# A planned attention and two gated layers on one core: the first gated item's gating, and the second item's products, moved into the attention's written order

## The chip, the cores and the metric

The kernel runs on one core of a Trainium2 chip. TensorE (PE in the profile) multiplies, VectorE (DVE), ScalarE (ACT) and GpSimd (POOL) do the element work, SyncE (SP) issues most of the transfers. The metric is the device time of one execution in microseconds (us); three runs give the median.

## The reference

Causal attention with a forgetting bias, four batches of eight heads, 576 tokens, head size 64; its output (2304 tokens by 512) goes through a sigmoid-gated layer (512 to 1536 and back) and then a cosine-gated layer (512 to 2048 and back). The weights arrive as 64-bit floats.

```python
cum = np.cumsum(np.maximum(s, 0), axis=-1)
bias = -(cum[:, :, :, None] - cum[:, :, None, :])
scores = np.where(causal, -1e9, q @ k.T / 8 + np.minimum(bias, 0))
x = softmax(scores) @ v                                     # 2304 x 512
x = (sigmoid(x @ w_gate) * (x @ w_val)) @ moe_w_out         # d_ff 1536
h = x @ w_in;  out = (h * cos(h)) @ moe2_w_out              # d_ff 2048
```

## The kernel before

**Attention.** The heads are worked in 16 pairs, p = 0 to 15, four pairs to a batch. All its steps are named operations, and one text, `SEQ`, writes them in a single order; each engine runs its own operations in the order in which that text names them, and `:a`, `:d`, `:p` choose ScalarE, VectorE or GpSimd where a step can run on several. `Plan.run` goes through the text once at build time and hands out buffers and PSUM banks with the durations that `add` states; it reorders nothing. The steps of a pair: `GQ`, `GK`, `GV`, `DB` load on SP (`GQT`, `GKT`, `GVT` the last 64 tokens of a whole batch); `PQ`, `PK` transpose on TensorE, `HQ`, `HK` copy that out; `A4`, `A3`, `A2`, `A0`, `A5` are scores; `ZT`, `ZA`, `Z`, `ZM` mask the bias; `X` is bias plus row maximum (VectorE, line 670), `E` the exponential (ScalarE, line 674), `T` and `C` the transposes (TensorE) and their copies (to `pt`); `V0`, `V1` the products with v (lines 744, 746). The sums go through `RA` (GpSimd), `RC` (VectorE), `RT` (TensorE) and `RR` to a row, `RD` stores the row to DRAM, `RB` reads it back spread over all partitions into the one tile `rb`; `U` copies the products of v out, `M` multiplies them by `rb`, and `XH`, `XL` (lines 449/445 and 788) split the result into two halves for the layers.

**Weights.** A piece of 128 by 512 64-bit numbers is fetched by SP into `raw` and turned into a high and a low half by `piece_ops`: exponent (VectorE, then a rebias on ScalarE, line 300), `mant_hi`, `mant_lo`, `sign` (VectorE, then an addition on GpSimd, line 313), `split` (VectorE, then a subtraction on GpSimd, line 321). The three pieces w0, w1, w2 of the first layer's first column block (gate, value, out) are decoded inside the attention's text. There an operation such as `exponent` issues its VectorE and its ScalarE instruction together, so that both stand at the same place of the text.

**Layers.** An item is one column block of 128 for one block of 384 tokens; a product takes three matmuls (`mm3`, lines 366 to 368) and an item's gate and value 24. `gate_val` makes both, `glu` takes the sigmoid (line 843), multiplies (844) and splits (846, 852), `down1` multiplies the item before by its out piece into banks 4 to 7, `evac1` collects. After item i the call `background` issues a share of the decoding of coming pieces: the first call, behind item 0, gives five operations, and the two fetches that they need. Of item 0 the 24 products `I0` to `I7` (three each) stand in the attention's text; its `glu` and all of the items after it come behind the text. The pool `att`, which holds the attention's tiles, is closed before the layers' pools are opened on the same memory.

```python
        attention()
        early.close()
        moe()
```

Of the kernel before, what the change touches and what calls it, by code (L numbers as in the profile page):

```python
# [10 lines left out]
F32 = mybir.dt.float32  # L11
# [58 lines left out]
class Banks(Pool):  # L70


    def pick(self, buf):
        best = (INF, 0, [])
        for i in range(0, self.n, 2):
            a, b = self.free[i], self.free[i + 1]
            if buf.n == 2:
                best = min(best, (max(a, b), 0, [i, i + 1]))
            else:
                for x, y, z in ((a, b, i), (b, a, i + 1)):  # L80
                    best = min(best, (x, -y if y < INF else -1e9, [z]))
        return best[0], best[2]
# [99 lines left out]
warm0 GQ0 tail cum table GKT0 GK0 GQT0 B0 BC0:d PK0 PQ0 Z0.0:p B1 out HQ0:a BC1:a ZT0.0 GK1 HK0:d A4.0 ZA0.0 GQ1 A0.0 X0.1.0 Z1.0:a PK1 DB1 ZT1.0 A3.0 GQ2 ZA1.0 X0.0.0  # L182
X1.1.0 HK1:a ZM1.3.0 X1.0.0 ZM0.3.0 A2.0 E0.1.0 X1.3.0 ZM1.2.0 PQ1 GK2 E1.1.0 E0.0.0 E1.0.0 HQ1:a X0.3.0 T0.1.0 ZT1.1 ZM0.2.0 T0.0.0 Z0.1:p X1.2.0 E1.3.0 ZM0.3.1 A5.0
X0.2.0 A4.1 Z1.1:p GQ3 C0.0.0:d DB2 GK3 ZA1.1 A0.1 E0.3.0 C0.1.0:d T0.3.0 X0.4.0 GV0 ZT0.1 GVT0 GKT4 A3.1 ZA0.1 E1.2.0 ZM1.3.1 E0.2.0 X1.0.1 E0.4.0 C0.3.0:d X0.0.1 T1.3.0
C1.3.0:a X1.1.1 X0.1.1 E0.1.1 PQ2 X0.3.1 ZM0.2.1 RA0 X1.3.1 PK2 HQ2:a T0.4.0 A2.1 E1.0.1 Z1.2:p HK2:d ZM1.2.1 Z0.2:p ZT0.2 ZM0.3.2 E1.1.1 C0.4.0:d E0.0.1 E0.3.1 T0.1.1
T0.0.1 T0.2.0 RC0 A5.1 ZT1.2 X0.2.1 X1.2.1 T1.2.0 X0.4.1 PQ3 C0.1.1:a C0.0.1:a PK3 C0.2.0:a ZA1.2 HQ3:a GQ4 C1.2.0:d A3.2 RT0 HK3:d E1.3.1 A4.2 GV1 T0.3.1 T1.3.1 ZA0.2
RR0:a X0.3.2 ZM1.3.2 E0.4.1 DB3 E1.2.1 X1.3.2 A0.2 X1.0.2 E0.2.1 X0.0.2 X1.1.2 V0.0 ZM1.2.2 X0.1.2 C0.3.1:a C1.3.1:d T0.2.1 E0.0.2 RD0 E1.0.2 T0.4.1 E1.3.2 GQT4 Z1.3:p
V1.0 C0.4.1:d T1.2.1 E1.1.2 T0.0.2 E0.1.2 ZM0.2.2 E0.3.2 U0:d C1.2.1:a ZT0.3 T0.1.2 ZT1.3 GK4 C0.2.1:a A5.2 C0.0.2:a A2.2 RA1 Z0.3:a RC1 A3.3 RB0 X0.4.2 X0.2.2 ZM0.3.3
X1.2.2 T0.3.2 GQ7 T1.3.2 C0.1.2:a ZM1.3.3 GV3 RT1 DB4 X0.3.3 GK5 V0.1 E0.4.2 X1.3.3 ZM1.2.3 ZA0.3 V1.1 ZA1.3 RR1:d M0:d PK4 ZM0.2.3 C1.3.2:d C0.3.2:d T0.4.2 E0.3.3 HK4:d
E1.3.3 U1:a E0.2.2 Z1.4:p PQ4 A4.3 HQ4:d ZT1.4 C0.4.2:a A0.3 X1.0.3 E1.2.2 XH0:p A2.3 Z0.4:p T0.2.2 X0.1.3 E1.0.3 E0.1.3 ZA1.4 X0.0.3 X1.1.3 T1.2.2 X1.2.3 ZM1.3.4 X0.2.3  # L190
T0.3.3 E0.0.3 T1.3.3 E1.1.3 T0.0.3 GV2 ZT0.4 C1.2.2:a ZA0.4 C1.3.3:d ZM0.3.4 C0.2.2:a E0.2.3 C0.3.3:d T0.1.3 A5.3 A3.4 GQT8 GQ5 RD1 X0.4.3 PQ5 RA2 C0.1.3:a C0.0.3:a A4.4
X0.3.4 DB5 A0.4 HQ5:a X1.3.4 E0.4.3 PK5 E0.3.4 V0.2 X1.1.4 X1.0.4 X0.0.4 ZM1.2.4 E1.0.4 RC2 GK6 HK5:d X0.1.4 T0.4.3 GK7 E1.3.4 RT2 RR2:d V1.2 Z1.5:p E1.2.3 E1.1.4
C0.4.3:d E0.1.4 ZM0.2.4 T0.2.3 Z0.5:p T1.2.3 E0.0.4 GQ6 U2:d RB1 A2.4 ZM1.3.5 RD2 T0.1.4 C1.2.3:a T0.0.4 ZT1.5 ZM0.3.5 GVT4 C0.2.3:a ZT0.5 X1.2.4 A5.4 T0.3.4 C0.0.4:a
# [37 lines left out]
def kernel(  # L231
# [847 lines left out]
```

## Time and profile before

| | us |
|---|---|
| median of three runs (1026.04 to 1028.54) | 1027.09 |
| the profiled execution, its own time | 1028.06 |
| its span, first to last instruction | 1026.3 |
| TensorE busy in the span | 1007.6 |
| VectorE, ScalarE, GpSimd busy | 709.7, 475.3, 411.2 |

The profiled execution's time stands 1.8 us above its span and 1.0 us above the median. Busy shares are means over three stages: the attention up to about 168 us, the first layer, and the second. Times in rows are from the span's start.

### The profile page before, as it was taken

What the parts mean: (1) busy time and instruction counts of PE and PEld (TensorE: products, weight loads), DVE (VectorE), ACT (ScalarE), POOL (GpSimd) and SP (SyncE); (2) the same over time, 40 slices, a digit from 0 to 9 for tenths busy, and PEclk for the clock granted to TensorE, in tenths of its full rate; (3) what the DMA queues carried; (4) which work ended last, traced back from release to release, by engine and by line L of the source; (5) the groups of instructions that cost most, each with busy time, mean ns of one, the idle gap of its engine ahead of it and who ended that gap; (6) DMA issues with size and microseconds to landing.
All of it is one profiled execution on the core that took longest, in us unless ns stands there. A gap on an engine that the chain in (4) does not pass through costs nothing.

```text
span 1026.3 us, 17410 instructions
## 1 busy us (share of the span) xinstructions
PE 1007.6 (98%) x6553; PEld 918.4 (89%) x6553; DVE 709.7 (69%) x1365; ACT 475.3 (46%) x1081; POOL 411.2 (40%) x489
## 2 busy tenths in 40 slices
PE   8999997999999999999999999999999999999998
PEld 5666665999999999999999999999999999999997
DVE  7878785655545557643345888987688878886565
ACT  6989894432222222221212335666555455554453
POOL 5478874432212223311112224565255535552222
PEclk9999998999999999999999999999999999999999
DMA  8776752311111112210101111211011101100011
GB/s 192 192 210 173 197 142 74 109 62 42 42 42 42 42 42 82 63 42 21 42 21 42 42 62 42 63 48 55 22 42 57 47 21 42 62 1 26 37 62 61
DMA packets 91508, 69.43 MB, mean 68 GB/s; under 512 B 58848, under 2 KB 79712, under 8 KB 91424
## 3 DMA queue, kind: packets, MB, share of 16 engines
q1 hardware_dynamic: 89792, 67.86, 23.2%
q8 instruction: 51, 0.84, 0.3%
q10 hardware_dynamic: 1632, 0.47, 0.2%
q14 instruction: 33, 0.27, 0.1%
HBM read 63.45 MB, written 4.87 MB: 67 GB/s over the span
## 4 chain that ended last, share of the span: by engine, by line
PE 90%; DVE 2%; DMA 2%; POOL 2%; ACT 2%; issue 1%; SPq 1%; DVEq 0%; POOLq 0%; ACTq 0%
PE pw L366 21%; PE pw L367 21%; PE pw L368 21%; PE pw L926 6%; PE pw L927 6%; PE pw L928 6%; PE pw L634 2%; DMA rb<-rec_d 2%; PE pw L746 1%; PE pw L456 1%; DVE pu L670 1%; ACT pu L674 1%; PE pw L639 1%; PE pw L560 1%; DMA Qn<-in_q_dram 1%
## 5 line engine op out<-in xcount | busy, mean ns | idle before, releaser
L366 PE MATMUL pw<-XH,wp 128*128 128x384 f32 x960 | 324.5, 338 | 5.6 <-ACT tm L843 4.8
L367 PE MATMUL pw<-XL,wp 128*128 128x384 f32 x960 | 324.2, 338 | 0.0
L368 PE MATMUL pw<-XH,wp 128*128 128x384 f32 x960 | 324.1, 338 | 0.0
L321 POOL TENSOR_TENSOR wp<-wm,wp 128x512 fp32r<-128x512 f32 x68 | 101.3, 1490 | 231.5 <-DVE wp L320 230.1
L366 PEld LDWEIGHTS pw<-XH,wp 128*128 128x128 f32 x960 | 181.2, 189 | 10.5 <-ACT tm L843 4.9
L367 PEld LDWEIGHTS pw<-XL,wp 128*128 128x128 f32 x960 | 181.2, 189 | 3.5
L368 PEld LDWEIGHTS pw<-XH,wp 128*128 128x128 f32 x960 | 181.2, 189 | 0.0
L916 POOL TENSOR_TENSOR gl<-tm,gh 128x384 fp32r<-128x384 f32 x96 | 109.3, 1138 | 144.4 <-ACT gh L915 144.3
L313 POOL TENSOR_TENSOR wm<-wm,wx 128x512 int32<-128x512 int32 x68 | 90.5, 1330 | 185.3 <-DVE wm L312 185.2
L844 DVE TENSOR_TENSOR tm<-pw,tm 128x384 f32<-128x384 f32 x72 | 40.1, 557 | 150.1 <-PE pw L368 140.0
L926 PE MATMUL pw<-wp,gh 128*128 128x512 f32 x288 | 112.2, 389 | 0.0
L927 PE MATMUL pw<-wp,gh 128*128 128x512 f32 x288 | 112.1, 389 | 0.0
L928 PE MATMUL pw<-wp,gl 128*128 128x512 f32 x288 | 112.0, 389 | 0.0
L846 ACT CAST gh<-tm 128x384 fp32r<-128x384 f32 x72 | 37.0, 514 | 145.3 <-DVE tm L844 145.3
L901 DVE SCALAR_TENSOR_TENSOR tm<-tm 128x384 f32<-128x384 int32 x96 | 99.2, 1033 | 3.3
L902 ACT ACTIVATE tm<-tm 128x384 f32<-128x384 f32 x96 | 50.5, 526 | 108.5 <-DVE tm L901 108.5
L367 PE MATMUL pw<-gl,wp 128*128 128x384 f32 x288 | 96.8, 336 | 0.0
L366 PE MATMUL pw<-gh,wp 128*128 128x384 f32 x288 | 96.5, 335 | 0.0
L300 ACT ACTIVATE wx<-wx,ebias 128x512 int32<-128x512 int32 x68 | 49.2, 724 | 102.1 <-DVE wx L299 101.0
L368 PE MATMUL pw<-gh,wp 128*128 128x384 f32 x288 | 96.2, 334 | 0.0
L674 ACT ACTIVATE pu<-pu,nm 128x128 f32<-128x128 f32 (+4 forms) x144 | 82.9, 579 | 4.7 <-DVE nm L670 4.4
L909 DVE SCALAR_TENSOR_TENSOR tm<-tm,pw 128x384 f32<-128x384 f32 x96 | 52.7, 549 | 42.4 <-ACT tm L903 42.4
(104 smaller groups left out, 1618.7 us busy)
## 6 DMA issues: line engine op xcount, KB each, us to landing
raw<-in_moe_w_out_dram SPq DMA_DIRECT2D x28, 512.0 KB
CB<-cum_d SPq DMA_DIRECT2D x15, 576.0 KB
raw<-in_moe_w_in_dram SPq DMA_DIRECT2D x16, 512.0 KB
raw<-in_moe_w_gate_dram SPq DMA_DIRECT2D x12, 512.0 KB
raw<-in_moe_w_val_dram SPq DMA_DIRECT2D x12, 512.0 KB
rb<-rec_d SPq DMA_DIRECT2D x32, 144.0 KB
out_dram<-acc SPq DMA_DIRECT2D x17, 256.0 KB
Kn<-in_k_dram SPq DMA_DIRECT2D x16, 256.0 KB
```

The costliest lines, as they stand in the source:

```text
L313: pool.tensor_tensor(m, m, st["x"], ALU.add)
L321: pool.tensor_tensor(w[:, 1], m, f(w[:, 0]), ALU.subtract)
L366: pe.matmul(ps, wh, xh, start=first, stop=False)
L367: pe.matmul(ps, wh, xl, start=False, stop=False)
L368: pe.matmul(ps, wl, xh, start=False, stop=last)
L674: act.activation(o, o, AF.Exp, bias=NMT[nm.slot][:, col:col + 1], scale=-1.0, accum_out=SUMS[sums.slot][:, col:col + 1])
L901: dve.scalar_tensor_tensor(r, kk, -TWO_PI_LO, r, ALU.mult, ALU.add)
L909: dve.scalar_tensor_tensor(g, r, -0.5, h, ALU.add, ALU.mult)
L916: pool.tensor_tensor(gl, g, f(gh), ALU.subtract)
L926: pe.matmul(ps, gh[:, ts], w[:, 0], start=it["first"], stop=False)
L927: pe.matmul(ps, gh[:, ts], w[:, 1], start=False, stop=False)
L928: pe.matmul(ps, gl[:, ts], w[:, 0], start=False, stop=it["last"])
```

## The change

Five edits. (1) `Buf` gets `fix`, so that a buffer can be tied to given banks: items 0 and 1 get banks 0, 1 and 2, 3. (2) The 24 products of item 1 (`I8` to `I15`) and the four gating instructions of item 0 (`Gs`, `Gm`, `Gh`, `Gl`) become operations of the attention's text; their tiles `TMA` and `GPA` lie in the pool `base`, and the layers' rings of tiles count on from there. (3) The decoding of w0, w1, w2 is listed instruction by instruction, with tiles `wx` and `wm` as buffers of the plan. (4) The Q and K tail tiles are one each instead of two. (5) Several stated durations change, and the text `SEQ` is another order throughout, with other choices of engine. In all 16 pairs, copies to `pt` go from 72 on ScalarE and 40 on VectorE to 65 and 47, `HK` from 8 and 8 to 13 and 3, `HQ` from 10 and 6 to 11 and 5, `RR` from 11 and 5 to 7 and 9, `U` from 6 and 10 to 7 and 9, `XL` from 14 on GpSimd and 2 on VectorE to 12 and 4; `M` stays 11 on GpSimd and 5 on VectorE.

```diff
 class Buf:
-    def __init__(self, pool, n=1):
+    def __init__(self, pool, n=1, fix=None):
+        self.fix = fix
...
     def pick(self, buf):
+        if buf.fix is not None:
+            return max(self.free[buf.fix:buf.fix + buf.n]), list(range(buf.fix, buf.fix + buf.n))
...
 SEQ = """
...
-C0.1.15:a GV15 C0.0.15:a RC13 E1.2.14 A3.15 T0.3.14 RT13 T1.3.14 GV14 X0.4.15 RR13:a E0.4.14 T0.2.14 X0.3.15 T1.2.14 A2.15 RD13 X1.3.15 ZM1.2.15 C1.3.14:a I0 ZM0.2.15
-E0.4.15 C0.3.14:d I1 I2 RA14 I3 I4 E0.3.15 X1.2.15 C1.2.14:d RC14 RT14 E1.3.15 X0.2.15 E1.2.15 T0.3.15 M12:p RR14:a w2fetch T1.3.15 C0.2.14:d E0.2.15 RA15 C1.3.15:a
-T0.4.14 T0.4.15 XH12:p C0.4.15:d RB13 XL12:p w2exponent I5 I6 RC15 I7 XL11:d RD14 T0.2.15 M13:d C0.4.14:a w2mant_hi RT15 T1.2.15 C0.3.15:a C0.2.15:a V0.14 w2mant_lo
-RR15:a V1.14 U14:d RD15 w2sign RB14 C1.2.15:a M14:d RB15 w2split V0.15 XH13:p XL13:p V1.15 XH14:a U15:d M15:d XL14:p XH15:d XL15:d
...
+A3.15 X0.1.15 X1.1.15 RB12 X1.0.15 E0.0.15 T1.3.14 I8 X1.3.15 E0.2.14 RA13 I9 E1.1.15 I10 E1.0.15 w1split_lo C0.3.14:d E0.1.15 I11 C1.3.14:a X0.3.15 RC13 T0.1.15 ZM0.2.15
+E0.4.14 RT13 w2mant_hi T0.0.15 RR13:d A5.15 X0.4.15 A2.15 C0.0.15:a RA14 RD13 w2exponent C0.1.15:a T0.2.14 T1.2.14 E1.3.15 M12:p X0.2.15 I0 I1 ZM1.2.15 X1.2.15 I12 I2 I13
+C0.2.14:d I14 E0.2.15 RC14 E0.4.15 T0.4.14 w2rebias w2mant_lo C1.2.14:a RB13 w2sign E0.3.15 GV15 C0.4.14:a RT14 I3 I15 T0.4.15 RR14:d RD14 E1.2.15 T0.2.15 T1.2.15 RA15 I4
+C1.2.15:a M13:p I5 C0.2.15:a I6 RC15 I7 XH11:p RT15 C0.4.15:d T0.3.15 RR15:a w2add_exp T1.3.15 Gs XH13:a w2split_hi C0.3.15:d V0.14 C1.3.15:d V1.14 Gm RD15 XH12:p RB14 Gh
+XL11:p Gl V0.15 V1.15 U14:a M14:p w2split_lo RB15 XH14:d XL14:d U15:a M15:d XH15:p XL12:p XL15:d XL13:d
 """
...
+    TMA = base.tile([P, TB], F32, name="tma")
+    GPA = base.tile([P, 2 * TB], F32R, name="gpa")
...
+        ops = [fetch, exponent, rebias, mant_hi, mant_lo, sign, add_exp, split_hi, split_lo]
+        if single:
+            return ops
...
-            QKT = {x: [att.tile([P, PB, 2, D], F32, name=f"{x}t{i}") for i in range(2)] for x in "QK"}
+            QKT = {x: [att.tile([P, PB, 2, D], F32, name=f"{x}t")] for x in "QK"}
...
+            for i, it in enumerate(items1[0:2]):
+                i_ps = Buf(pl["pw"], 2, 2 * i)
+                i_ps.left += 1
+                for y in range(2 * NDC):
+                    def part(u, z=y // NDC, c=y % NDC, it=it, i_ps=i_ps):
+                        it["ps"] = [PW[:, i_ps.slot + y, 0:it["n"]] for y in range(2)]
+                        xmm(it["ps"][z], W["gv"[z], it["f"]], it["o"], it["n"], [c])
...
+                add("Gs", "act:1780", glu_s, rd=[(i_ps, 0), *[("e", NP - 1, c) for c in range(NS)], *[("e", NP - 2, c) for c in range(NS)]], wr=["g0"])
+                add("Gm", "dve:550", glu_m, rd=[(i_ps, 1)], wr=["g0"])
+                add("Gh", "act:510", glu_h, rd=["g0"], wr=["gh0"])
+                add("Gl", "dve:560", glu_l, rd=["g0", "gh0"], wr=["gl0"])
...
-            TM = mid.tile([P, 5 * TB], F32, name="tm")
-            gp = c2.enter_context(tc.tile_pool(name="gp", bufs=4))
+            TMB = mid.tile([P, 4 * TB], F32, name="tmb")
+            GPB = mid.tile([P, 6 * TB], F32R, name="gpb")
...
             for i, it in enumerate(items1):
+                if i > 1:
+                    gate_val(it)
                 if i > 0:
-                    gate_val(it)
                     for c in range(NDC):
                         down1(items1[i - 1], c)
-                glu(it)
+                    glu(it)
                 if i > 0:
                     evac1(items1[i - 1], 0)
                     evac1(items1[i - 1], 1)
-                glu_lo(it)
                 if i > 0:
+                    glu_lo(it)
```

## Rows read from the trace of the kernel before

**Rows 1.** Windows view, three stretches: engines' busy time, granted TensorE clock, DMA share.

```profile
168.00:172.50 4.50, 0.00 (x0) 0.00 (x0) 1.76 (x3) 2.43 (x3) 1.99 (x3) 0.84 0.25 50
172.50:181.50 9.00, 8.10 (x24) 7.59 (x25) 4.95 (x8) 0.89 (x3) 2.69 (x2) 0.51 0.37 125
...
187.80:560.00 372.20, 372.20 (x2147) 372.20 (x2146) 202.98 (x377) 89.16 (x172) 91.65 (x65) 1.00 0.15 46
```

**Rows 2.** Timeline of TensorE, 166 to 188 us: start, duration, line; idle before.

```profile
167.49 0.28 PE L746 MATMUL pw<-pt,vt 128*64 128x64 f32 x4
172.57 0.69 PE L366 MATMUL pw<-XH,wp 128*128 128x384 f32 x1 [4.79 <-ACT tm L843]
177.61 0.69 PE L366 MATMUL pw<-XH,wp 128*128 128x384 f32 x1 [0.83 <-DVE tm L844]
181.50 0.34 PE L366 MATMUL pw<-gh,wp 128*128 128x384 f32 x1
...
187.74 0.34 PE L366 MATMUL pw<-gh,wp 128*128 128x384 f32 x1
```

**Rows 3.** Windows view, the attention from 16 to 163 us, sum: PE, PEld, DVE, ACT, POOL.

```profile
sum 147.00, PE 140.06 PEld 92.87 DVE 119.63 ACT 131.71 POOL 103.51; mean PE 35.01 PEld 23.22 DVE 29.91 ACT 32.93 POOL 25.88
```

**Rows 4.** Waits of ScalarE, 50 to 100 us, then 140 to 163 us: total, times, longest.

```profile
ACT wx L300 <- DVE wx L299: 2.1, 1, 2.1
...
ACT wx L300 <- DVE wx L299: 1.1, 1, 1.1
```

**Rows 5.** Waits of GpSimd, 16 to 163 us.

```profile
POOL w L776 <- DMA rb<-rec_d: 3.9, 4, 2.1
```

**Rows 6.** Groups by line and form, 0 to 168 us: busy us, mean ns of one.

```profile
L788 POOL TENSOR_TENSOR XL<-w,XH 128x576 fp32r<-128x576 f32 x12 | 17.8, 1485 | 0.8 <-DVE XH L449 0.4
...
L445 ACT COPY pt<-pw 128x384 f32<-128x384 f32 x25 | 11.0, 477 | 0.9 <-PE pw L456 0.7 <-DVE pt L449 0.2
...
L445 ACT COPY K<-pw 128x640 f32<-128x640 f32 x8 | 5.6, 696 | 1.0 <-PE pw L560 0.9
```

**Rows 7.** Timeline of ScalarE, 155 to 174 us and 168 to 192 us.

```profile
162.49 0.25 ACT L445 COPY rr<-pw 9x128 f32<-9x128 f32 x1
...
170.73 1.28 ACT L843 ACT_TABLE_LOAD   x1
...
183.90 0.47 ACT L843 ACTIVATE tm<-pw 128x384 f32<-128x384 f32 x1
```

**Rows 8.** Timeline of SP, 155 to 180 us: issues.

```profile
162.76 0.58 SPq L765 DMA_DIRECT2D rec_d<-rr  x1
...
164.12 7.00 SPq L770 DMA_DIRECT2D rb<-rec_d  x4
177.22 0.38 SPq L295 DMA_DIRECT2D raw<-in_moe_w_gate_dram  x1
```

**Rows 9.** Waits of SP's queue, 165 to 180 us.

```profile
SPq L295 <- DVE XL L788: 6.0, 1, 6.0
...
SPq L770 <- DMA rb<-rec_d: 2.1, 1, 2.1
```

**Rows 10.** Timeline of VectorE, 168 to 192 us.

```profile
169.25 0.76 DVE L776 TENSOR_TENSOR w<-w,rb 128x576 f32<-128x576 f32 x1 [2.68 <-DMA rb<-rec_d]
...
173.89 1.91 DVE L776 TENSOR_TENSOR w<-w,rb 128x576 f32<-128x576 f32 x1 [2.88 <-DMA rb<-rec_d]
...
176.33 0.76 DVE L788 TENSOR_TENSOR XL<-w,XH 128x576 fp32r<-128x576 f32 x1
...
180.68 0.43 DVE L299 TENSOR_SCALAR wx<-raw 128x512 int32<-128x512 int32 x1 [1.86 <-DMA raw<-in_moe_w_gate_dram]
...
185.54 0.56 DVE L852 TENSOR_TENSOR gl<-tm,gh 128x384 fp32r<-128x384 f32 x1 [0.58 <-ACT gh L846]
```

**Rows 11.** The tile rb over the span: count, duration ns min/median/max.

```profile
L776 POOL TENSOR_TENSOR w<-w,rb x11: 1405/1416/1432, 51.8 to 155.5; 128x576 f32<-128x576 f32 x11
L776 DVE TENSOR_TENSOR w<-w,rb x5: 735/758/1909, 34.5 to 173.9; 128x576 f32<-128x576 f32 x5
```

More of the change, by code (lines that the diff above doesn't have):

```diff
@@ new lines @@
+E0.2.10 A2.11 GQT12 GQ12 ZM0.2.11 ZM1.2.11 ZA0.11 X0.1.11 RR9:a X0.0.11 XL6:p T0.2.10 X1.0.11 X1.1.11 E0.0.11 Z1.12:p RB8 w0rebias RA10 T1.2.10 E0.1.11 ZT0.12 V0.9
+C1.2.10:d E1.1.11 C0.2.10:d X1.2.11 V1.9 E1.0.11 PQ12 X0.2.11 T0.1.11 E0.3.11 ZT1.12 U9:d T0.0.11 E1.3.11 HQ12:a A5.11 PQ13 RC10 A3.12 Z0.12:p GK15 C0.1.11:d RD9 E0.2.11
+HQ13:a w1fetch ZA0.12 C0.0.11:d GQ14 X0.4.11 E1.2.11 DB13 ZM1.3.12 ZM0.3.12 T0.3.11 E0.4.11 X0.3.12 RT10 XH7:p RR10:d A4.12 ZA1.12 w0add_exp T1.3.11 XL7:p C0.3.11:a
@@ L287, with piece_ops @@
     raw_pool = [wraw]
[L289 removed]
+    def piece_ops(src, e, dst, key, single=False):
         st = {}
@@ L312, in sign, with add_exp, split_hi, split_lo @@
             dve.scalar_tensor_tensor(m, st["raw"][:, :, 1], -2**31, m, ALU.bitwise_and, ALU.bitwise_or)
+        def add_exp():
+            m = st["m"]
             pool.tensor_tensor(m, m, st["x"], ALU.add)
-        def split():
+        def split_hi():
             ring = w0ring if npiece[0] % 16 < 3 else rings[0]
             npiece[0] += 1
-            w = ring.tile([P, 2, 512], F32R, name="wp")
-            m = st["m"].bitcast(F32)
-            dve.tensor_copy(w[:, 0], m)
-            pool.tensor_tensor(w[:, 1], m, f(w[:, 0]), ALU.subtract)
-            dst[key] = w
-        return [fetch, exponent, mant_hi, mant_lo, sign, split]
+            st["w"] = dst[key] = ring.tile([P, 2, 512], F32R, name="wp")
+            dve.tensor_copy(st["w"][:, 0], st["m"].bitcast(F32))
+        def split_lo():
+            w = st["w"]
+            pool.tensor_tensor(w[:, 1], st["m"].bitcast(F32), f(w[:, 0]), ALU.subtract)
+        ops = [fetch, exponent, rebias, mant_hi, mant_lo, sign, add_exp, split_hi, split_lo]
+        if single:
+            return ops
+        def both(name, *parts):
+            def run():
+                for x in parts:
+                    x()
+            run.__name__ = name
+            return run
+        return [fetch, both("exponent", exponent, rebias), mant_hi, mant_lo, both("sign", sign, add_exp), both("split", split_hi, split_lo)]
     def col_piece(w, i):
@@ L483, in setup_tail @@
             def setup_tail(u):
-                for i in range(2):
-                    for e in range(2):
-                        u.memset(QKT["Q"][i][half(1 - e), :, e], 0.0)
-                    u.memset(QKT["K"][i][half(0)], 0.0)
+                for e in range(2):
+                    u.memset(QKT["Q"][0][half(1 - e), :, e], 0.0)
+                u.memset(QKT["K"][0][half(0)], 0.0)
                 for i in range(NPU[4]):
@@ L790, in attention @@
                     continue
-                W0 = {"fetch": "sp:620", "exponent": "dve:1000 ", "rebias": "act:730", "mant_hi": "dve:640", "mant_lo": "dve:810", "sign": "dve:900", "add_exp": "pool:1340",
-                      "split_hi": "act:613 dve:443", "split_lo": "pool:1490"}
-                for z, ops in enumerate(w1_ops(0)):
-                    raw = Buf(pl["raw"])
+                W0 = {"fetch": "sp:550", "exponent": "dve:430", "rebias": "act:640", "mant_hi": "dve:420", "mant_lo": "dve:700", "sign": "dve:690", "add_exp": "pool:1280",
+                      "split_hi": "dve:440", "split_lo": "pool:1280"}
@@ L797, in attention @@
+                for z, ops in enumerate(w1_ops(0, True)):
+                    raw, wx, wm = Buf(pl["raw"]), Buf(pl["wx"]), Buf(pl["wm"])
+                    use = {"fetch": ([("xl", W0AT)], [raw]), "exponent": ([raw], [wx]), "rebias": ([], [wx]), "mant_hi": ([raw], [wm]), "mant_lo": ([raw], [wm]), "sign": ([raw], [wm]),
+                           "add_exp": ([wx], [wm]), "split_hi": ([wm], [("W", z, 0)]), "split_lo": ([wm, ("W", z, 0)], [("W", z, 1)])}
                     for op in ops:
                         n = op.__name__
-                        dur = {"fetch": "sp:520", "exponent": "dve:500", "mant_hi": "dve:800", "mant_lo": "dve:1400", "sign": "dve:700", "split": "dve:450"}[n]
@@ L800, in attention @@
-                        add(f"w{z}{n}", dur, lambda u, op=op: op(), rd=[raw] if n != "fetch" else [("xl", W0AT)], wr=[raw] if n != "split" else [raw, ("W", z)], xfer=1.9 if n == "fetch" else 0.0)
-            it = items1[0]
-            i_ps = Buf(pl["pw"], 2)
-            i_ps.left += 1
-            for i in range(2 * NDC):
-                def part(u, z=i // NDC, c=i % NDC):
-                    it["ps"] = [PW[:, i_ps.slot + y, 0:it["n"]] for y in range(2)]
-                    xmm(it["ps"][z], W["gv"[z], it["f"]], it["o"], it["n"], [c])
-                add(f"I{i}", "pe:520", part, rd=[("W", i // NDC), *[(y, x) for y in ("xh", "xl") for x in range(PB)]], wr=[i_ps])
+                        rd, wr = use[n]
```

155 lines of the change are left out of this document (88 added, 67 removed).

## The prediction

> **What bounds the kernel now.** I read the windows view first. From 187.8 us on TensorE is busy without a break at the full clock, 372.2 of 372.2 us [rows 1]; none of the edits alters a product there, so that part keeps its time. What can move is the attention and the passage from it to the layers. In the passage the same view shows no product from 168 to 172.5 us and then a granted clock of 0.51, the lower level (1.2 GHz), until 181.5 [rows 1]. The timeline of TensorE gives the places: the attention's last product starts at 167.49, ending at about 167.77; item 1's gate starts at 172.57 behind item 0's sigmoid (same banks), its value at 177.61 behind item 0's multiply; item 0's down products start at 181.50, item 1's at 187.74 [rows 2]. From 181.50 to 187.74 are 36 products, 0.173 us each; from 177.61 to 181.50 are 12, 0.324 each.
>
> In the attention the fullest element engine is ScalarE: 131.7 of 147 us, against 119.6 on VectorE and 103.5 on GpSimd [rows 3]. TensorE shows 140.1, but the ends of its products are modelled; counted by the distances of its starts in the timeline, its work up to the last `RT` is some 133 us, and that instruction starts at 161.7 us. So an order is worth what it saves ScalarE in waits, 15.3 us in all.
>
> **What the passage seems to offer.** After the attention's last product the old order does item 1's 24 products, then 12 down, then 24 for item 2: it reaches item 1's down products 20.0 us after 167.77. The new one has 36 left, 6.2 us at full clock. If nothing else bound, that would give 13.7 us. I do not forecast it, because of what item 1's own gating waits for.
>
> **The chain that I think binds.** The layers' first fetch of weights started at 177.22 [rows 8], 0.13 us after VectorE's last attention instruction (`XL15`, 176.33 + 0.76) [rows 10]; the wait view says so, 6.0 us on that line [rows 9]. Its target lies on old bias tiles, free by then, so the fetch waits for the whole closed pool. From there the order, in both kernels, is: fetch, the five decoding operations of the first `background` call, and only then item 1's `glu`, since all three stand in that order on VectorE and ScalarE. Measured: 177.09 to the first decoding at 180.68; item 1's sigmoid at 183.90 behind the second rebias; its low half starts at 185.54 and ends at 186.10 [rows 7, 10]. That is 9.0 us from the end of the attention's last VectorE instruction, call it e, to the item's low half. Before, TensorE came to item 1's down products only at 187.74, 1.6 us later, and the chain was hidden. After, TensorE is there early and the chain is what is late next.
>
> **Where e comes to stand.** I count from r, the start of `RR15`: 162.49 before [rows 7], so e was r + 14.6 and item 1's down products r + 25.25. Both texts then put `RD15` ahead of `RB14` on SP, so `RB14` starts at r + 1.63 (164.12, rows 8). It landed 5.1 us later, 2.1 of them a wait for an earlier transfer on the queue; `RB15` took 3.9 from the end of `M14` (170.01) to 173.89 [rows 9, 10]. New sum: `RB14` 4.5 (3.9 to 5.1), r + 6.15. `M14` is on GpSimd now: 1.42 instead of 0.76 [rows 11], r + 7.6. `RB15` 4.3 with its hand-over, r + 11.9. `M15` on VectorE 0.75, r + 12.6. `XH15` moves to GpSimd, about 0.7 and 0.2 of hand-overs, r + 13.5. Then VectorE has two subtractions, `XL15` and `XL13`, where it had one, while GpSimd does `XL12`. Alone they are 1.5; beside GpSimd one such instruction of VectorE took 1.91 (`M15`) instead of 0.76. I take 2.3 (1.5 to 2.9): e = r + 15.8. Adding 9.0 and 0.1, item 1's down products start at r + 24.9, against r + 25.25: 0.35 us gained, no more.
>
> A rule speaks against the change here. The Trainium skill (SBUF — State Buffer, Who interferes with whom) says that a VectorE instruction with two SBUF inputs and a GpSimd instruction that reads SBUF lock each other out whole. By it the end of the text would be `XL12`'s 1.49 and then 0.76 twice, 3.0 instead of my 2.3, and the forecast 0.7 us later. The 1.91 us row agrees with it.
>
> **The clock.** TensorE ends its attention products at r + 5.3, waits for `w2split_lo` behind `M14` (r + 7.6 + 1.28, r + 8.9), does item 0's down products and item 2's 24, at most 8 us with part of it at the low level, and stands from about r + 17 to r + 24.9. In the old trace a stand of 4.8 us was enough to bring the clock to 0.5 [rows 1, 2]. So the first 12 products behind the gap take 3.9 instead of 2.1 us, 1.8 lost; from 0 (clock stays) to 3.6 (two such groups). Passage together: 1.8 - 0.35 = 1.45 us later, if r stays.
>
> **The attention's order (r).** Loads hardly differ. Copies to `pt`, by type: ScalarE loses 1, 1 and 6 of the three shortest and gains 1 of 512 columns, some -3.4 us at about 0.48 each [rows 6]; it gains five `HK` and one `HQ` at 0.70, +4.2; the other shifts bring it to about -0.3. VectorE gets about +1.2, GpSimd -2.2 (two `XL` fewer at 1.49, some `XH` more) and 1.2 us less memset of tail tiles at the start, which hides under the first products. TensorE gets 24 products more, 4.2 us: they stand where its work of 133 us leaves 28 us of waits, so 0, but up to 4.2 if the end of the order is TensorE's. Of item 0's gating, 2.3 us on ScalarE and 1.1 on VectorE stand ahead of `U14`, hidden under the 5.6 us of `V0.14` to `V1.15`; item 0's sigmoid no longer holds TensorE. The stated durations only choose buffers: nothing.
>
> What the order can save: in the old text the rebias stands right behind its exponent, and ScalarE stood 2.1 and 1.1 us at two of the three [rows 4]; listed apart, these 3.2 us can go. GpSimd waited 3.9 us at `M` for `rb` [rows 5]. Between `RB` and `M`, summed over TensorE's work, the old text leaves 2.6 us on average for p up to 13, twice 0.0; the new one 3.4, once under 0.5. The nearest loads stand at a distance of 0.0, 1.7 and 1.8 before, 3.1 after the start phase. Single tail tiles could cost: a batch's tail cannot load before the last pair of the old batch is transposed, and `GQT12` leaves only 3.2 us of TensorE's work until `PQ12`, under the 4 to 5 us of a transfer; 0 to 2 us. I take 4.0 saved: the 3.2, and 0.8 of the GpSimd waits. Bounds: 8 (half of ScalarE's 15.3), and a loss of 4, as much in new waits as I take off.
>
> **Sum.** 1028.06 - 4.0 + 1.45 = 1025.5 for a profiled execution. That one stood 1.0 above the median of its runs, so 1024.5 for the median, 2.6 us faster.
>
> **Rivals.** *The passage pays in full.* If the fetch waited only for the bytes that it overwrites, the five decoding operations (2.6 us on VectorE) would have their data, the 3.6 us from 177.09 to 180.68 would fall out of the 9.0, and item 1's low half would end about 5.5 us behind e, at r + 21.3: 3.6 us better, 1020.9. For it: item 0's operations have been taken out of the chain. Against it: the 6.0 us wait [rows 9].
>
> *Nothing is gained.* The order removes the ScalarE waits and finds others; saved 1.5 instead of 4.0: 1027.0. For it: ScalarE was at 90% already [rows 3].
>
> *Slower: GpSimd blocks the last pair.* In the new text `M12:p` stands ahead of the mask `ZM1.2.15`, and `RB12` only 0.9 us of products behind `A3.15`; in the old one `M12` stood behind all masks. `M12` waits for 4 to 5 us of transfer and runs 1.42; `X1.2.15`, `E1.2.15`, `RA15` and r follow it. ScalarE has other work for some 9 us after `A3.15`, so it decides once `M12` ends more than about 8 us after `A3.15`, one late `RB12` of 1.5 us. Its price is the lateness, up to a transfer and an `M`, 6.5; I take 5.5: 1030.0. Against it: GpSimd's transfer waits were at most 2.1 us [rows 5].
>
> **Chances and range.** Forecast 0.34, paid in full 0.12 (with it all that ends faster: 0.46), nothing gained 0.30, slower 0.24. What a measurement can tell from no change is about 0.2%, 2 us. The forecast's own range is 1021.5 to 1026.5. For 8 in 10 it has to reach the far side of the full payment and most of the slower case: 1019.5 to 1030.5.
>
> **What would show it.** SP's first layer fetch right behind VectorE's last `XL`, and some 9 us from there to item 1's low half: the chain is right. A stand of TensorE of several us ahead of item 1's down products, clock 0.5 behind it: the clock term. `RR15` near 158.5 us: the order's gain; later than 162.5, the slower rival, if `M12` is seen waiting for `rb`. The prediction is wrong if TensorE goes through without a stand, or if the new order costs what it was to save.

## The result, and the profile after

The new kernel takes 1032.74 us (median of 6 runs, 1030.85 to 1034.85), the kernel before 1026.57 beside it: a ratio of 1.006 (95% interval 1.0042 to 1.0078). Forecast were 1024.5 and a range up to 1030.5, so it came out on the slower side and outside the range. The profiled execution took 1032.08 (span 1030.3), 4.0 more than that of before. The medians lie 6.2 apart, not 4.0, because the profiled execution of before stood 1.5 us above the median of 1026.57 and that of the new kernel 0.7 below its own.

Windows view of the new kernel, columns as in [rows 1]; the first row reaches to the start of `RR15`, the second from pair 14's first `X` to pair 15's last `E`:

```profile
0.00:164.47 164.47, 155.95 (x1937) 103.31 (x1939) 130.00 (x408) 140.12 (x410) 109.56 (x253) 1.00 0.75 178
...
139.10:161.30 22.20, 22.20 (x230) 15.81 (x226) 17.72 (x54) 18.03 (x55) 14.07 (x23) 1.00 0.41 117
...
173.30:180.00 6.70, 6.49 (x19) 5.98 (x20) 4.39 (x5) 0.64 (x1) 2.06 (x2) 0.50 0.14 43
...
189.20:193.50 4.30, 4.30 (x14) 4.30 (x15) 3.33 (x6) 1.84 (x5) 2.78 (x2) 0.50 0.04 6
198.00:560.00 362.00, 362.00 (x2089) 362.00 (x2088) 194.99 (x364) 84.74 (x163) 87.84 (x62) 1.00 0.15 46
```

Timeline of TensorE, with the idle time before an instruction in brackets (against [rows 2]):

```profile
170.70 0.34 PE L391 MATMUL pw<-gpa,wp 128*128 128x384 f32 x1
...
173.27 0.69 PE L392 MATMUL pw<-gpa,wp 128*128 128x384 f32 x1 [2.23 <-POOL wp L335]
...
189.16 0.66 PE L390 MATMUL pw<-gpb,wp 128*128 128x384 f32 x1 [6.30 <-issue]
...
210.02 0.34 PE L390 MATMUL pw<-gpa,wp 128*128 128x384 f32 x1
```

ScalarE (against [rows 7]), SP and its wait (against [rows 8, 9]), VectorE (against [rows 10]):

```profile
164.47 0.26 ACT L469 COPY rr<-pw 9x128 f32<-9x128 f32 x1 [1.58 <-PE pw L480]
...
187.07 0.47 ACT L898 ACTIVATE tmb<-pw 128x384 f32<-128x384 f32 x1
```

```profile
166.09 7.01 SPq L793 DMA_DIRECT2D rb<-rec_d  x4
179.88 0.37 SPq L301 DMA_DIRECT2D raw<-in_moe_w_gate_dram  x1
```

```profile
SPq L301 <- DVE XL L811: 6.7, 1, 6.7
```

```profile
175.59 0.76 DVE L799 TENSOR_TENSOR w<-w,rb 128x576 f32<-128x576 f32 x1 [1.26 <-DMA rb<-rec_d]
177.11 2.64 DVE L811 TENSOR_TENSOR XL<-w,XH 128x576 fp32r<-128x576 f32 x2 [0.76 <-POOL XH L473]
183.86 0.43 DVE L305 TENSOR_SCALAR wx<-raw 128x512 int32<-128x512 int32 x1 [4.11 <-DMA raw<-in_moe_w_gate_dram]
...
188.71 0.56 DVE L907 TENSOR_TENSOR gpb<-tmb,gpb 128x384 fp32r<-128x384 f32 x1 [0.58 <-ACT gpb L901]
```

The reader should see two things. The passage goes as its chain was told: the fetch starts 0.13 us behind VectorE's last `XL` (177.11 + 2.64 = 179.75), the decoding at 183.86, item 1's sigmoid at 187.07, its low half ends at 189.27, and TensorE, idle for 6.3 us, starts item 1's down products beside that end, at 189.16. But the attention does not end earlier: `RR15` starts at 164.47, where 158.5 was forecast and 162.49 was before [rows 7].

From `RR15` (r, as in the prediction) to the first down product of item 4, behind which TensorE works without a break in both, the new kernel takes 210.02 - 164.47 = 45.55 us and the old one 206.48 - 162.49 = 43.99. Between these two profiles the passage costs 1.56 us, forecast 1.45. The other 1.98 us of 3.54 are r. The old kernel's line:

```profile
206.48 0.34 PE L366 MATMUL pw<-gh,wp 128*128 128x384 f32 x1
```

### The profile page after: what moved, and what is told of

The parts are those of the page before. It is cut to its first block, busy times and chain, and to the rows that moved or that the text cites. A ratio compares the mean times of both kernels' runs of the same rounds, so it can differ in the third digit from the quotient of the medians.

```text
span 1030.3 us, 17409 instructions
## 1 busy us (share of the span) xinstructions
PE 1009.3 (98%) x6553; PEld 917.7 (89%) x6553; DVE 712.0 (69%) x1372; ACT 476.9 (46%) x1075; POOL 409.5 (40%) x485
## 4 chain that ended last, share of the span: by engine, by line
PE 91%; issue 3%; POOL 2%; DVE 1%; ACT 1%; DMA 1%; SPq 0%; POOLq 0%; DVEq 0%; ACTq 0%
PE pw L390 21%; PE pw L391 21%; PE pw L392 21%; PE pw L982 6%; PE pw L981 6%; PE pw L983 6%; PE pw L657 2%; PE pw L769 2%; PE pw L480 2%; PE pw L662 1%; DMA rb<-rec_d 1%; PE pw L583 1%; ACT pu L697 1%; POOL CB L502 1%; DVE pu L693 0%
## 5 line engine op out<-in xcount | busy, mean ns | idle before, releaser
L971 POOL TENSOR_TENSOR gpb<-tmb,gpb 128x384 fp32r<-128x384 f32 x72 | 82.6, 1147 | 110.6 <-ACT gpb L970 110.6
L899 DVE TENSOR_TENSOR tmb<-pw,tmb 128x384 f32<-128x384 f32 x57 | 31.7, 557 | 120.2 <-PE pw L392 114.1
L982 PE MATMUL pw<-wp,gpb 128*128 128x512 f32 x216 | 84.1, 389 | 0.0
L981 PE MATMUL pw<-wp,gpb 128*128 128x512 f32 x216 | 84.1, 389 | 0.0
L983 PE MATMUL pw<-wp,gpb 128*128 128x512 f32 x216 | 84.0, 389 | 0.0
L390 PE MATMUL pw<-gpb,wp 128*128 128x384 f32 x216 | 73.2, 339 | 6.3 <-issue 6.3
L391 PE MATMUL pw<-gpb,wp 128*128 128x384 f32 x216 | 73.3, 340 | 0.0
L392 PE MATMUL pw<-gpb,wp 128*128 128x384 f32 x216 | 72.9, 337 | 0.0
L321 DVE SCALAR_TENSOR_TENSOR wm<-raw,wm 128x512 int32<-128x512 int32 x68 | 71.1, 1046 | 1.6
L950 ACT ACTIVATE tmb<-pw 128x384 int32<-128x384 f32 x96 | 46.5, 484 | 37.8 <-PE pw L392 37.6
L901 ACT CAST gpb<-tmb 128x384 fp32r<-128x384 f32 x43 | 22.1, 514 | 88.7 <-DVE tmb L899 88.7
L898 ACT ACTIVATE tmb<-pw 128x384 f32<-128x384 f32 x57 | 27.8, 487 | 72.6 <-PE pw L392 72.6
```

Source lines behind the costliest of these rows:

```text
L321: dve.scalar_tensor_tensor(m, st["raw"][:, :, 1], -2**31, m, ALU.bitwise_and, ALU.bitwise_or)
L390: pe.matmul(ps, wh, xh, start=first, stop=False)
L391: pe.matmul(ps, wh, xl, start=False, stop=False)
L392: pe.matmul(ps, wl, xh, start=False, stop=last)
L971: pool.tensor_tensor(gl, g, f(gh), ALU.subtract)
L981: pe.matmul(ps, gh[:, ts], w[:, 0], start=it["first"], stop=False)
```

## The experiments

Each was timed in five rounds beside the kernel before; ratios are to that kernel, with 95% intervals. Diffs are against the new kernel unless the text says otherwise.

### The passage

**Decoding behind the gating.** Both kernels, with no `background` call behind item 0 (the five operations join the next call):

```diff
-                if id(it) in share:
+                if i > 0 and id(it) in share:
```

> The changed kernel with one edit: the first background call (five decoding operations and the two fetches) is issued behind item 1's gating instead of ahead of it. Theory A (the new wait is the chain: end of VectorE's attention work at 179.75, fetch, five decoding operations, then item 1's gating, 9.5 us): item 1's low half ends about 2 us behind 179.75, TensorE arrives at 182.86 and does not stand, item 1's down products start near 183 instead of 189.16, and the second fall of the clock (2.1 us) goes too: 6 to 8.4 us faster than the changed kernel, 1024 to 1026.5. Theory B (the loss lies in the attention's new order alone): no change, 1032.7. Theory C (the decoding is what the layer needs early): slower than 1032.7, TensorE waits for weights at item 6.

> The kernel before with the same single edit as a control. Theory A: there the chain ended 1.6 us ahead of TensorE (186.10 against 187.74), so nothing changes, within 1 us of 1026.6. If decoding ahead of the gating costs by itself, some us faster; if early decoding is needed, slower.

The new kernel: 1029.40, 1.0028 (1.0017 to 1.0038), slower than the forecast of 1024 to 1026.5. Item 1's down products start at 181.26 instead of 189.16, so the five operations were in the chain. But ten now stand ahead of item 2's gating, and the stand moves there:

```profile
192.46 0.69 PE L390 MATMUL pw<-gpb,wp 128*128 128x384 f32 x1 [4.67 <-ACT acc L927]
```

The kernel before: 1024.63, 0.9987 (0.9974 to 1.0000). By the ratio that is 1.3 us less, a little over the 1 us that was allowed for, but not clear of no change; this fits a chain that was covered there, and does not prove it.

**The decoding shared out from item 1 on**, in place of from item 0:

```diff
-                    group = [x for x in items1 if x["gi"] == it["gi"]][min(it["gi"], 1):]
+                    group = [x for x in items1 if x["gi"] == it["gi"]][1:]
```

> The changed kernel with the first group's 30 decoding operations shared out over items 1 to 5, six each, instead of items 0 to 5, five each: none stands ahead of item 1's gating, and six instead of ten stand ahead of item 2's. Theory A (fetch and decoding ahead of a gating set TensorE's stand; in the run with all ten behind item 1 the stand only moved to item 2): item 1's down products near 181 to 183, item 2's near 188, no stand over 2 us, 8 to 9.5 us faster than the changed kernel, 1023 to 1025. Theory B (attention's order alone): no change. Theory C (the layer needs the decoding early): no better than the run with all ten behind item 1, 1029.4.

1024.13, 0.998 (0.9967 to 0.9992). Timeline of VectorE: item 1's low half is now ahead of the first decoding.

```profile
179.62 0.56 DVE L907 TENSOR_TENSOR gpb<-tmb,gpb 128x384 fp32r<-128x384 f32 x1 [0.58 <-ACT gpb L901]
181.43 0.43 DVE L305 TENSOR_SCALAR wx<-raw 128x512 int32<-128x512 int32 x1 [1.25 <-DMA raw<-in_moe_w_gate_dram]
```

From r to item 4's down products: 37.2 us instead of 45.55. One index brings back some 8 us (8.4 in this passage).

**The fetch made free.** The raw tiles get a pool of their own that lies only on the attention's raw tile:

```diff
...
-            st["x"] = raw_pool[0].tile([P, 512], I32, name="wx")
+            st["x"] = raw_pool[-1].tile([P, 512], I32, name="wx")
...
-            st["m"] = raw_pool[0].tile([P, 512], I32, name="wm")
+            st["m"] = raw_pool[-1].tile([P, 512], I32, name="wm")
...
+            raw_pool[0] = c2.enter_context(tc.tile_pool(name="rawp", bufs=2))
...
-            raw_pool[0] = c2.enter_context(tc.tile_pool(name="wraw2", bufs=2))
+            raw_pool.append(c2.enter_context(tc.tile_pool(name="wraw2", bufs=2)))
```

> The changed kernel with the layers' two raw tiles in a pool of their own that lies exactly on the old decoding pool, so that the first fetch waits for the last decoding of w2 instead of for the whole attention pool. Order of all engines unchanged. Theory A: fetch near 173.3 instead of 179.9, its data is there when VectorE ends at 179.75, and item 1's low half ends 5.5 us behind that instead of 9.5: 4 us faster, up to 6 if the stand gets too short for the clock to fall; 1026.7 to 1028.7. Rival (the wait is the five decoding operations alone): no change.

1026.74, 1.0009 (0.9998 to 1.0021). SP fetches at 172.49 instead of 179.88, and the low half ends 5.6 us behind e instead of 9.5; the prediction's first rival put "about 5.5". Its mechanism was right; what kept it from coming true is the wait for the closed pool.

```profile
172.49 0.49 SPq L301 DMA_DIRECT2D raw<-in_moe_w_gate_dram  x1
```

**Item 1's products behind the attention**, in their old place:

(`I8` to `I15` also go out of the text.)

```diff
...
-            for i, it in enumerate(items1[0:2]):
+            for i, it in enumerate(items1[0:1]):
...
-                if i > 1:
+                if i > 0:
                     gate_val(it)
```

> The changed kernel with item 1's 24 products taken out of the attention's text again and put behind it, item 0's gating staying inside. Theory A with a TensorE-bound drain: RR15 goes back by about 2 us to 162.5, the 24 products run in the time in which TensorE stood, and item 1's down products start near 187.2: about 2 us faster, 1030.7, with the stand still there. Theory B (the order elsewhere costs): no change. If the products inside the text are worth their 4.2 us: slower by 2 to 4.

1031.68, 1.0051 (1.0036 to 1.0065), no change clear of noise against the new kernel. A stand of some 7 us stays, and from r to item 4's down products it takes 44.1 us, 1.4 less: behind the attention these products fill TensorE's wait for `w2split_lo`, inside the text they don't. I first took the earlier `RR15` (163.51) as a gain in the last pairs; the windows row below says that it is not.

### The order

**The kernel before, with the decoding listed by instruction** (nine operations a piece, the rebias behind `mant_hi`; w1 and w2 likewise, the rest of its text unchanged):

```diff
-w0mant_hi E0.1.8
+w0mant_hi w0rebias E0.1.8
...
-w0sign E0.0.11
+w0sign w0add_exp E0.0.11
...
-w0split PQ12
+w0split_hi w0split_lo PQ12
```

> The kernel before with the decoding of w0 to w2 listed by instruction, rebias one operation later than the exponent, everything else in its old place. The prediction's order term (3.2 us of ScalarE's waits at the rebias come back): 2.5 to 3.5 us faster than before, 1023.5 to 1024.5. Theory of the traces (those waits go and others take their place, because ScalarE, VectorE and TensorE are all nearly full): within 1 us, 1026 to 1028.

1022.73, 0.9968 (0.9957 to 0.9979), and `RR15` at 158.74, 3.75 us earlier. Windows view:

```profile
0.00:158.74 158.74, 151.22 (x1927) 100.58 (x1929) 126.70 (x398) 139.12 (x417) 112.08 (x258) 1.00 0.73 185
...
136.00:155.60 19.60, 18.60 (x229) 13.06 (x227) 15.21 (x49) 17.60 (x58) 14.87 (x27) 1.00 0.39 119
```

ScalarE's idle time up to `RR15` is 158.74 - 139.12 = 19.6 us here and 23.6 before (162.49 - 138.87 in the same view): 4.0 us, the prediction's amount to a tenth, although the prediction had only 3.2 of it from ScalarE. In the new kernel it is 164.47 - 140.12 = 24.35. ScalarE waits at no rebias there either, but its other idle time grew by more. Listing alone has the gain; the rest of the new order gives it back, with 1.25 us of work on top.

Where: starts of pair 14's and pair 15's first `X`, end of pair 15's last `E`, and `RR15`, from the timelines (us, one profile for each row):

| | X of 14 | X of 15 | last E of 15 | RR15 | X of 14 to last E |
|---|---|---|---|---|---|
| before | 139.0 | 146.9 | 158.7 | 162.5 | 19.7 |
| listed | 136.0 | 143.9 | 155.6 | 158.7 | 19.6 |
| new | 139.1 | 150.4 | 161.3 | 164.5 | 22.2 |
| new, item 1's products behind | 136.7 | 148.1 | 159.0 | 163.5 | 22.3 |
| new up to pair 14, then old | 140.4 | 148.3 | 159.8 | 162.9 | 19.4 |

The last column is 21.9 to 22.3 in nine profiles with the new order in the last pairs and 19.4 to 19.8 in nine with the old: 2.6 us are lost there, all of it ahead of pair 15's first `X` (11.4 us behind pair 14's, against 7.9); from there to the last `E` the new order is 0.8 shorter. Up to pair 14, twelve profiles of the new text start at 136.7 to 140.4, on average 138.2, two of the old at 138.6 and 139.0: some 0.6 gained of the 2.8 that listing has there, in its one profile. Against that profile the twelve are 2.2 us late at pair 14, and 1.1 us already at pair 1's first `X` (on average 17.2 us, listed 16.1), ahead of any load that waits for a tail tile. In between, the difference falls below 0.5 (pairs 5 and 12) and rises again. What makes it is not known.

**The last turn earlier**: `C0.4.15 RC15 RT15 RR15` ahead of `I4`.

> The changed kernel with the last pair's reciprocal turn (C0.4.15, RC15, RT15, RR15) moved in the text ahead of I4 to I7, four groups of products. Theory A with a TensorE-bound drain: RR15 starts near 163.0 instead of 164.47, the end of VectorE's attention work and item 1's down products move with it: 1.0 to 1.8 us faster, about 1031.3. If the drain is bound by ScalarE or by transfers: no change.

1030.65, 1.0038 (1.0026 to 1.0051): as forecast; `RR15` comes 1.7 us behind the last `E` instead of 3.1.

**Single tails in the listed old order**: one Q and one K tail tile as in the new kernel, each load behind the last transpose from the tile that it overwrites (shortened; `GQT8` goes behind `PQ7` in the same way).

```diff
-... GV0 GVT0 GKT4 PQ2 PK2 PQ3 PK3 GQ4 ... PQ10 GQT12 RB5 ... PQ11 RB6 ... PK11 PK12 ...
+... GV0 GVT0 PQ2 PK2 PQ3 PK3 GKT4 GQ4 ... PQ10 RB5 ... PQ11 GQT12 RB6 ... PK11 GKT12 PK12 ...
```

> The kernel before with the decoding listed by instruction (1022.7 us in its own experiment) and, besides, the single Q and K tail tiles; the tail loads are moved behind the last use of the tile that they overwrite, the rest of the order stays. If the single tails are what the new order lost up to pair 14: the K tail of the last batch comes too late, TensorE stands 1 to 3 us, 1024 to 1026 us. If the order itself lost it: tails cost nothing, 1022.2 to 1023.2 us, last row of sums (RR15) within 0.4 us of 158.7.

1038.54, 1.0123 (1.0103 to 1.0142): neither; 15.8 us slower than without. Waits of SP's queue (total, times, longest), then of TensorE:

```profile
SPq L559 <- PE pw L580: 8.3, 1, 8.3
...
SPq L556 <- PE pw L580: 3.7, 1, 3.7
```

```profile
PE pw L580 <- DMA Kn<-in_k_dram: 4.1, 2, 2.9
PE pw L580 <- DMA Kt<-in_k_dram: 1.6, 1, 1.6
```

SP stands at the tail loads (Q's is line 559, K's 556) with the other loads queued behind: TensorE waits longer for whole K than for the tail itself. With the loads put later on the queue (behind `RD0`, `DB7`, `PK11`; `PK12` behind `RD9`):

> The kernel before, decoding listed (1022.7 us in its own experiment, its RR15 at 158.7 us), single Q and K tail tiles as in the first attempt with them (1038.5), but the tail loads stand later on SP's queue: behind RD0, behind DB7 and behind PK11, with PK12 moved behind RD9, so that SP does not stand at a tail load with other loads behind it. If single tails cost only where SP waits for the old tail's last transposes: 1022 to 1024.5 us, RR15 by 160. If one tile is late wherever its load is placed: over 1027 us, TensorE seen waiting for Kt or Qt.

1028.59, 1.0028 (1.0018 to 1.0038), `RR15` at 164.95: 10 us come back, 5.9 stay. By its time that is the rival, but no product waited for a tail; ScalarE stood 2.6 us at a copy to `rr` whose store of the row before was late on SP. In the new order no product waited for a tail either, and SP stood 5.1 us at the tail loads; what they cost there was not tried.

**The new order up to `A4.14`, the old from there**, item 1's products behind, decoding shared out from item 1, fetches free:

> The new order up to pair 14's first scores (A4.14), from there on the rest in the old text's order, item 1's products behind the attention; decoding shared out from item 1 and fetches free, as in the run above. If the new order loses some 3 us up to pair 14 against the listed old one, and 2 to 3 more in its last two pairs: pair 14's first X near 139 us, RR15 near 162.5, 2.5 to 4.5 us slower than the run above with all three if that has RR15 at 159, and 1019 to 1022 us in all. If all the loss lies in the last two pairs: RR15 at 160 or earlier, within 1.5 us of it.

1019.81, 0.9937 (0.9919 to 0.9955), the lowest median of all (its interval overlaps that of 1021.33 below) and 12.9 us under the new kernel's. `RR15` at 162.92, forecast 162.5. TensorE has no stand behind the attention, and the clock stays at 1.00:

```profile
166.00:170.00 4.00, 4.00 (x30) 2.89 (x27) 3.42 (x7) 0.51 (x1) 1.89 (x2) 1.00 0.24 70
170.00:175.00 5.00, 5.00 (x31) 5.00 (x30) 1.83 (x2) 0.68 (x1) 4.59 (x4) 1.00 0.55 173
```

**What makes the 2.6 us of the last pairs?** Three single causes were tried. In the new kernel's row above TensorE is full, 22.20 of 22.20; without item 1's products it is not, and the stretch is as long:

```profile
136.70:159.00 22.30, 18.66 (x216) 12.33 (x212) 18.13 (x54) 17.98 (x55) 14.08 (x23) 1.00 0.39 116
```

So not these products. Next, ScalarE's waits for `RR12` and for VectorE's decoding (`E0.3.14`, `E1.3.14` ahead of `RR12`; w2's operations behind the last `X` or `E`):

> The new kernel with seven of its operations moved in the last two pairs: E0.3.14 and E1.3.14 ahead of the copy RR12, into a stand of ScalarE of 1.9 us; w2's mant_hi and exponent behind the last X, and its rebias, mant_lo and sign behind the last E of pair 15. From pair 14's first X to pair 15's last E this stretch took 22.2 us in the new kernel and 22.3 with item 1's products taken out, against 19.7 in the kernel before. If ScalarE's waits for TensorE's RT12 and for VectorE's decoding make the difference: 20 us or less, RR15 2 to 3 us earlier against pair 14's first X, 1029.5 to 1031.5 us in all. If TensorE's products set it: 22 us as before, 1032 to 1034.

1031.72, 1.006 (1.0042 to 1.0079). The waits for `RR12` fall from 1.9 to 0.5 us, and the stretch is 22.0 (137.6 to 159.6): not these. Last, the place of pair 15's scores: the old text has `PQ15`, `A4.15`, `A0.15` ahead of `V0.13` and `V1.13`, the new one behind, so I moved them (on the kernel with item 1's products behind, item 0 in banks 2 and 3):

> The new kernel with item 1's products behind the attention (1031.7 us) and pair 15's transposes and first scores (PQ15, HQ15, A4.15, A0.15), its first masks and its first four X, ahead of V0.13 and V1.13, as the text before had them; item 0 in banks 2 and 3. In the new order V0.13 and V1.13 stand ahead of them, 3.4 us of TensorE. If this place makes the 2.6 us: pair 15's first X 8 to 8.8 us behind pair 14's (11.4 in all new orders, 7.9 in the old ones), last E of pair 15 19.5 to 20.5 us behind it (22.3), 1028.5 to 1030 us in all. Rival, ScalarE or VectorE holds the second half: first X earlier, last E still 21.5 us or more behind, 1031 us or more.

1035.48, 1.0097 (1.0078 to 1.0115): slower. The move did not reach its end. VectorE waited 3.2 us for a mask of GpSimd, which has `XL10` and `M11` ahead of it on its own list:

```profile
144.15 1.42 POOL L814 TENSOR_TENSOR XL<-w,XH 128x576 fp32r<-128x576 f32 x1
145.53 0.29 POOL L505 TENSOR_SCALAR_AFFINE_SELECT CB<-CB 128x128 f32<-128x128 f32 x1
145.79 1.40 POOL L802 TENSOR_TENSOR w<-w,rb 128x576 f32<-128x576 f32 x1
147.14 1.28 POOL L505 TENSOR_SCALAR_AFFINE_SELECT CB<-CB 128x128 f32<-128x128 f32 x5
```

```profile
147.96 0.29 DVE L696 CUSTOM_DVE_ANT_0 pu<-pw,CB 128x128 f32<-128x128 f32 x1 [3.24 <-POOL CB L505]
```

Pair 15's first `X` came 10.4 us behind pair 14's, not 8 to 8.8, and the last `E` 24.6. So this theory is neither shown nor refuted. The loss is placed (the old text from `A4.14` on takes it away), but no one operation was found that makes it: that stays open.

### Edits put together

Decoding shared out from item 1, fetches free, last turn earlier:

> The changed kernel with the three edits together: shares from item 1, the fetch freed from the attention pool, the last reciprocal turn ahead of I4. Theory A: item 1's down products near 181.5, item 4's near 200.5 against 210.0 in the changed kernel and 206.5 before: 1022 to 1023.5, 4 to 5 us faster than the kernel before. Theory B: about 1030.6, as with the earlier turn alone.

1021.94, 0.9965 (0.9954 to 0.9977). With the seven moves of the last pairs besides:

> The same seven moves on the kernel with the decoding shared out from item 1, the free fetches and the earlier last turn (1021.9 us). If the waits make the difference: the stretch takes 20 us or less and the total is 1019 to 1020.5 us. If TensorE sets it: 22 us and 1021.5 to 1023.

1021.33, 0.9954 (0.9942 to 0.9965): the same within the intervals; the stretch is 21.9. The listed old order with single tails (first placement) and item 0's gating inside, then also with decoding shared out and fetches free, then this with moved tails:

> As the experiment with single tails, and item 0's four gating instructions inside the written order, on the tiles of the new kernel; item 1's products behind the attention. Theory of the chain (item 1's gating ends some 9.3 us behind VectorE's last attention instruction, whatever item 0 does): item 1's down products at about 181.5 us against 182.4 without it, TensorE stands 5 to 7 us ahead of them and the clock falls behind the stand, 1022 to 1025 us. Rival: item 0's gating held TensorE, so moving it pays on its own: item 1's down products near 176 us, 1016 to 1018 us.

> The same with both other edits: the layers' decoding shared out from item 1 on, and its fetches on a tile of their own that waits for no attention tile. Theory of the chain: nothing is left between VectorE's last attention instruction and item 1's gating, item 1's down products at about 175 us, no stand over 2.5 us, 1014.5 to 1018 us. Rival: the gating and the last split ahead of M14 on VectorE push the attention's end back by 2 us or more, or TensorE waits for item 1's own split: 1019 to 1022 us.

> The order of the experiment with moved tails, with item 0's gating inside the text (its products in banks 6 and 7), decoding shared out from item 1 on, and the layers' fetches on a tile of their own. From the earlier run of these edits: item 4's down products 34.8 us behind RR15. With RR15 at 158.7 to 160: 1013.5 to 1017 us. Rival: RR15 stays as late as with the first placement (near 165 or later): above 1020 us.

1038.98, 1.0127 (1.0106 to 1.0149); 1030.27, 1.0041 (1.0025 to 1.0058); 1026.18, 1.0001 (0.9991 to 1.0011). All three totals missed, since the tails' cost came with them. The passage did as told in two: gating inside alone (with w2's last split ahead of `M14`) leaves a stand of 6.6 us and 43.3 us from r to item 4's down products; with the other two edits it is 34.8. With moved tails (item 0 in other banks) it is 37.0, and `RR15` came at 166.2. Item 0's gating pays nothing clear while item 1's hangs on the fetch; with the fetch free and the decoding behind, the passage is 8.6 us shorter. What those two edits give without the gating inside was not tried. The last one, the moved scores with both edits of the passage:

> As the run above, with the decoding shared out from item 1 and the free fetches. If the place of the scores makes the 2.6 us: 1018 to 1020 us, the fastest but for chance. Rival: 1021 us or more.

1026.01, 0.9996 (0.9982 to 1.0009): the rival, as with the scores alone.

## Why the prediction was wrong

**The passage's chain was right; that its price fits is in part luck.** `RB14` started at r + 1.62 (forecast 1.63), `M14` at r + 6.1 (its data forecast at 6.15), the last `XL` ended at r + 15.3 (15.8), item 1's low half came 9.5 us behind it (9.0), the down products at r + 24.7 (24.9). The two subtractions took 2.64 us, between my 2.3 and 3.0. By the rule of the Trainium skill (SBUF — State Buffer, Who interferes with whom) the prediction's estimate was 3.0, and the trace leans to it: GpSimd's `XL12` ended at 178.47, and two instructions of 0.76 behind that would end at 179.99, measured 179.75. TensorE's wait for `w2split_lo` ended at r + 8.8 (8.9). The clock term was 1.8 and came to 2.1 (item 1's down products 1.42 us late, item 2's 3.54).

But all of this was counted from one profile of the old passage, and that one was at the long end. Where the same passage stood in other kernels (the listed one and the two with single tails), it took 42.4, 42.9 and 40.8 us, not 43.99, and VectorE's last `XL` ended at r + 13.1 to 13.5, not r + 14.6. The new passage took 45.55 and, with the waits in the last pairs mended, 45.2. Against those three profiles it costs some 3 us, not 1.56. The forecast of 1.45 met the one old profile that it was made from.

**The step that failed is the order term**, "I take 4.0 saved". `RR15` came 1.98 us later, 6.0 us off the forecast, out of the 6.6 us by which the profiled execution missed 1025.5. (The median missed by 8.2; the other 1.7 are that the profiled execution was taken to stand 1.0 above its median and stood 0.7 below.) The amount belonged to one edit: listing the decoding saved 3.75 us when made alone. I credited the new order with it and charged the rest of the order nothing. Against the listed kernel, the new one's `RR15` is 5.7 us late: 3.1 up to pair 14 (2.2 on the average of the twelve profiles) and 2.6 in the last two pairs. Which operations lose it stays open. GpSimd's waits for `rb`, of which 0.8 was to go, went from 3.9 [rows 5] to 7.1 us:

```profile
POOL w L799 <- DMA rb<-rec_d: 7.1, 3, 4.4
```

**"TensorE gets 24 products more, ... so 0"** held: without them the stretch is no shorter. "Up to 4.2 if the end of the order is TensorE's" looks true in the new trace, TensorE full to 164 us, and experiment says no. **Single tails, "0 to 2 us"**, were sized too small for an order not made for them, 5.9 to 15.8; for the new one this is not known.

**The rivals.** `M12` (154.88) waited for no transfer and did not hold up the last pair. "Nothing is gained" was nearest, and its mechanism (ScalarE's waits at the rebias go, others come) is what ScalarE shows, but its 1027.0 still gave the order 1.5 us. My own bound, a loss of 4, gives 1028.06 + 4 + 1.45 = 1033.5 for a profiled execution and 1032.5 for the median; the range stopped at 1030.5, at the slower rival's price. It should have gone at least to the bound.

## What to carry to other kernels

When a change replaces a whole written order, its gain cannot be read from the waits it removes: price the edit that removes them (here the listing) by itself, and give the rest of the reordering a range with the same weight on a loss. A TensorE that shows no gap is not yet the bound: taking 24 products out of a full stretch left it 22.3 us long. Where a load on an in-order queue must wait for a buffer, count what is queued behind it: here placing such loads later brought back 10 of 15.8 us. And a passage that is counted from one profile has that profile's luck in it: the old one took 40.8 to 44.0 us from kernel to kernel.

## What was not expected of the hardware

Behind a stand of TensorE of 2.23 us the new kernel's clock was 0.50 from 173.3 to 180 us; with the decoding behind the gating, a stand of 1.83 us at the same place left it at 1.00 from 173 to 180. The length of the stand does not decide it alone: in the kernel with moved tails, item 0's gating inside and both edits of the passage a stand of 2.35 us left the clock at 1.00 (first row), and with the decoding shared out from item 1 it was 0.50 behind stands of 1.96 and 0.90 us (second row).

```profile
174.00:178.00 4.00, 4.00 (x23) 4.00 (x24) 1.08 (x1) 0.00 (x0) 3.83 (x4) 1.00 0.68 229
...
172.00:178.00 6.00, 5.12 (x16) 5.12 (x17) 3.48 (x4) 0.68 (x2) 2.06 (x2) 0.50 0.06 20
```

And one text gave, up to pair 14, starts 3.7 us apart from profile to profile (136.7 to 140.4), while the stretch behind it repeated within 0.4; 2.2 of the 3.7 are there at pair 1's first `X` (16.4 to 18.6). A single profile prices that first part no closer.
